# A linear-attention layer with an MLP on one core: batches 2 and 3 turn their first 384 tokens through memory, and their attention stands earlier in the order

## The chip, the cores and the metric

The kernel runs on one core of a Trainium2 chip. Time is device time in microseconds (us) of one execution. The core has TensorE (PE in the profile; its weight loads are PEld), VectorE (DVE), ScalarE (ACT), GpSimd (POOL), and SyncE (SP), whose only work here is to issue transfers.

## The reference, cut to what matters

```python
# r, k, v: (4, 8, 768, 48) f32; w, u: (8, 48)
for t in range(S):                                   # a state D x D for each batch and head
    cur = einsum('bhd,bhe->bhde', u[None] * kt, vt)
    y[:, :, t] = einsum('bhd,bhde->bhe', rt, state + cur)
    state = w[None, :, :, None] * state + einsum('bhd,bhe->bhde', kt, vt)
x = y.transpose(0, 2, 1, 3).reshape(4, 768, 384)
h = x.transpose(0, 2, 1) @ U @ V                     # U (768, 32), V (32, 768)
u = x + h.transpose(0, 2, 1)
out = u + maximum(u @ w_ch1, 0) @ w_ch2              # 384 -> 1536 -> 384
```

## The kernel before, in words

Each batch of 768 tokens is worked in six chunks of 128 tokens for the attention, and in two halves (t = 0 and 1) of 384 tokens for the MLP. The attention of batch b+1 runs between the matmuls of batch b's MLP, so that TensorE has work all the time.

**The order.** Every operation is given a key (a time in us, `at(t, f)`), and `Plan.schedule` (L152) walks through a modelled execution: on each engine it takes, among the operations whose inputs and buffers are ready by its own estimates, the one with the smallest key. The result is a fixed order for each engine, SyncE's queue among them; on the chip each engine works its list in that order and waits wherever an input is not there yet. `begin[b]` (L1456) is the key at which batch b's MLP begins, 49 x 1.85 apart. The MLP of a batch is 48 units of nine 384-wide matmuls, 1.85 apart in key (`mlp_units`, L1335): `m_1(f)` makes 128 of the 1536 hidden rows from u (L1257), ScalarE and VectorE split the result into a high and a low part (hh, hl), and `m_2(f)` (L1277) multiplies them with the second weights. For batches 1 to 3 the half t = 0 is done first (24 units), then t = 1.

**Attention.** `attention(b, t0, per, lead, step)` (L1473) gives chunk c the key t0 + per * c. For batches 2 and 3, t0 is begin[b-1] + 8 and per is 11, so that it ends at begin[b-1] + 74. Loads are keyed behind them: `a_load` (rows of r, k, v into tiles ldr, ldk, ldv, vsw) at the chunk's key less per and 16, `a_load_blocks` (r and k of three chunks as 32 x 32 blocks into tile bl, in runs of 128 bytes, 32 transfers) at the first chunk's key less per and 18. VectorE turns the blocks (L773), and scales them (L775, either VectorE or GpSimd). The chunk itself is `a_chunk` (L1050): products on TensorE whose first instruction is at L854; its two sums on VectorE make tile x, in token order.

**From attention to MLP.** `c_g(b)` (L1144) sums U against all six tiles x into Gs (32 rows, kept in three parts for accuracy), over TensorE, ScalarE and VectorE. What the MLP needs is u = x + h transposed, as a high part uTh and a low part uTl. There are two ways:

- *inside* (t = 0 of every batch, and t = 1 of batch 0): `c_x` (L1182) turns the three tiles x on TensorE against the identity into three PSUM banks (tiles pu, bank_sc, bank_tr), nine 128 x 128 transposes; `c_xu` (L1196) adds h to each bank by one matmul of Gs and V and splits the bank into uTh and uTl. Tile x stays without h, so that `m_2` of f = 0 adds h to the output by three more matmuls (*gates*, L1293).
- *through memory* (t = 1 of batches 1 to 3): `c_u` (L1168) makes h of one tile by one matmul and VectorE adds it to x; `c_store` (L1227) writes the tile to memory (tile ud) in runs of 128 bytes, so that 32 x 32 blocks stand turned; `c_blocks` (L1234) loads 128 rows of the turned array (tile ub); `c_turn` (L1240) turns the inside of the blocks on VectorE (tile ut) and splits into uTh and uTl. Both transfers are issued by SyncE.

The keys of both stand at the end of `rwkv_moe` (L1500 to L1532).

Of the kernel before, what the change touches and what calls it, by code (L numbers as in the profile page):

```python
# [47 lines left out]
class Plan:  # L48
# [33 lines left out]
    def op(self, eng, ns, fn, w=(), r=(), alt=(), lock=False, dma=0.0, rows=0, late=0.0, tiled=False, dk=0.0):  # L82


        if self.direct:
            fn()
            return None
        o = Op()
        o.n = len(self.ops)
        o.key = (self.key + dk, o.n)  # L90
        o.ways = [(eng, ns, fn, lock)] + list(alt)
        o.dma, o.rows, o.late, o.tiled = dma, rows, late, tiled
        o.deps, o.behind, o.allocs, o.bufs = set(), set(), [], []
        for acc, write in [(a, False) for a in r] + [(a, True) for a in w]:
            b, sub = acc if isinstance(acc, tuple) else (acc, None)
            if not b.uses and b.tag:
                o.allocs.append(b)
                ring = self.rings.setdefault(b.tag, {"order": [], "next": 0, "free": [(-99.0, "")] * b.bufs, "last": None})
                ring["order"].append(b)
            elif b.tag and b.uses[0][0] is not o:  # L100
                o.behind.add(b.uses[0][0])
            for p, s, pw in b.uses:
                if (write or pw) and (s is None or sub is None or s == sub) and p is not o:
                    o.deps.add(p)
            b.uses.append((o, sub, write))
            if b not in o.bufs:
                o.bufs.append(b)
                b.left += 1
        self.ops.append(o)
        return o  # L110
# [191 lines left out]
def rwkv_moe(ctx: ExitStack, tc: tile.TileContext, r, k, v, w, u, U, V, w1, w2, out):  # L302
    nc = tc.nc
    B, H, S, D = r.shape
    C = 128
    NCH = S // C
# [8 lines left out]
    NCT = DM // 128  # L315
# [3 lines left out]
    TPB = TB // 128  # L319
# [29 lines left out]
    def bank(tag, name):  # L349
        made = Buf(ps, [128, 512], F32, tag, {"mm": 2, "acc": 3}.get(tag, 1), name)  # L350
        if tag in ("tr", "sc"):
            if tag not in lasting:
                lasting[tag] = ps.tile([128, 512], F32, name=f"bank_{tag}", tag=tag, bufs=1)
            made.got = lasting[tag]
        return made
# [7 lines left out]
    def whole(*args, **kw):  # L363

        opened.clear()
        return nc.tensor.matmul(*args, **kw)  # L366

    def pe(ns, fn, w_, r_, tiled=False, dk=0.0):
        return op("PE", ns, fn, w_, r_, tiled=tiled, dk=dk)
# [16 lines left out]
    def dma(fn, w_, r_, rows, run, eng="SP", ns=470, dk=0.0, late=0.0, either=False):  # L386

        q = nc.scalar if eng == "ACT" else nc.sync
        return op(eng, ns, lambda: fn(q), w_, r_, dma=rows * max(1.05, run / 320),
                  rows=rows, late=late, dk=dk, alt=[("ACT", ns, lambda: fn(nc.scalar), False)] if either else ())  # L390
# [266 lines left out]
    xs = {}  # L657
# [510 lines left out]
    def c_u(b, i):  # L1168
        n = b * NCH + i

        pt = bank(("tr", "sc", "av")[i % 3], f"ph_{n}") if b < B else bank("mm", f"ph_{n}")
        pe(174, lambda: whole(pt.t[:, :DM], lhsT=V3.t[:, i * 128:(i + 1) * 128], rhs=Gs[b].t, start=True, stop=True),
           [pt], [V3, Gs[b]])
        on_dve(384, lambda e: e.tensor_tensor(xs[n].t, pt.t[:, :DM], xs[n].t, ALU.add), [xs[n]], [pt])
# [2 lines left out]

    def inside(b, t):

        return b < B and (t == 0 or b == 0)  # L1180

    def c_x(b, t, i):  # L1182

        if i == 0:
            upt[b, t] = [bank("acc" if (b, t) == (0, 0) else ("sc", "av", "tr")[ct], f"pu{b}_{t}_{ct}") for ct in range(NCT)]
        x = xs[b * NCH + t * TPB + i]
        for ct in range(NCT):
            pe(115, lambda ct=ct: whole(upt[b, t][ct].t[:, i * 128:(i + 1) * 128], lhsT=x.t[:, ct * 128:(ct + 1) * 128],
                                        rhs=ident_, start=(i == 0), stop=False, is_transpose=True, skip_group_check=True),
               [upt[b, t][ct]], [x])  # L1190
# [5 lines left out]
    def c_xu(b, t):  # L1196
        u_bufs(b, t)
        uh, ul = uT[b, t]
        for ct in range(NCT):
            pt = upt[b, t][ct]  # L1200
            pe(200, lambda ct=ct, pt=pt: whole(pt.t[:, :TB], lhsT=Gs[b].t[:, ct * 128:(ct + 1) * 128],
                                               rhs=V3.t[:, t * TB:(t + 1) * TB],
                                               start=False, stop=True, skip_group_check=True), [pt], [Gs[b], V3])
            on_act(384, lambda ct=ct, pt=pt: nc.scalar.copy(uh.t[:, ct, :], pt.t[:, :TB]), [(uh, ct)], [pt])
            on_dve(384, lambda e, ct=ct, pt=pt: e.tensor_tensor(ul.t[:, ct, :], pt.t[:, :TB], f32(uh.t[:, ct, :]),  # L1205
                                                                ALU.subtract), [(ul, ct)], [pt, (uh, ct)])
# [17 lines left out]
    ud_pool = ctx.enter_context(tc.tile_pool(name="ud", bufs=1, space=bass.MemoryType.DRAM))  # L1224
    ud = [Buf(ud_pool, [NCH, DM // 32, 32, 128], F32, None, 1, f"ud{b}") for b in range(B)]

    def c_store(b, i):  # L1227
        dma(lambda q: q.dma_start(ud[b].t[i].rearrange("k t (m c) -> (t m) k c", c=32),
                                  xs[b * NCH + i].t.rearrange("p (k c) -> p k c", c=32)), [(ud[b], i)], [xs[b * NCH + i]],
            1536, 128, ns=470)  # L1230

    ublk = {}

    def c_blocks(b, t, ct):  # L1234

        bt = ublk[b, t, ct] = wbuf([128, TPB, 128], F32, "xh", NXS, f"ub_{b}_{t}_{ct}")
        dma(lambda q: q.dma_start(bt.t, ud[b].t[t * TPB:(t + 1) * TPB, 4 * ct:4 * ct + 4].rearrange("j k t e -> (k t) j e")),
            [bt], [(ud[b], i) for i in range(t * TPB, (t + 1) * TPB)], 384, 512, late=1000)

    def c_turn(b, t, ct):  # L1240
        if ct == 0:
            u_bufs(b, t)
        uh, ul = uT[b, t]
        bt = ublk.pop((b, t, ct))
        ut = wbuf([128, TB], F32, "xl", NXS, f"ut_{b}_{t}_{ct}")
        on_dve(680, lambda e: e.transpose(ut.t.rearrange("p (j t m) -> p j m t", t=32, m=4),
                                          bt.t.rearrange("p j (m c) -> p j m c", c=32)), [ut], [bt])
        on_act(384, lambda: nc.scalar.copy(uh.t[:, ct, :], ut.t), [(uh, ct)], [ut])  # L1248
        on_either(384, lambda e: e.tensor_tensor(ul.t[:, ct, :], ut.t, f32(uh.t[:, ct, :]), ALU.subtract), [(ul, ct)],  # L1249
                  [ut, (uh, ct)])  # L1250
# [178 lines left out]
    def at(t, f):  # L1429
        steps.append((t, len(steps), f))  # L1430
# [25 lines left out]
    begin = [T0 + 49 * PER * b for b in range(B)]  # L1456
# [40 lines left out]
    end = attention(0, FRONT, EACH, 2.0, 0)  # L1497
    for i in range(3):
        at(end + 0.1 + 0.1 * i, lambda i=i: c_x(0, 0, i))
    for b in range(B):  # L1500
        n0 = b * NCH
        last = b + 1 == B
        t = begin[b]
        if b:
            t0, per = ((begin[b - 1] + 34, 8.0), (begin[b - 1] + 8, 11.0))[b > 1]
            for c in range(NCH):
                at(t0 + per * c - per - 16, lambda n=n0 + c: a_load(n))
            for c in range(0, NCH, 3):
                if turned(n0 + c):
                    continue  # L1510
                for i in (1, 3, 0, 2):
                    at(t0 + per * c - per - 18 + 0.1 * i, lambda n=n0 + c, i=i: (a_load_blocks(n, i, 0), a_load_blocks(n, i, 1)))
            end = attention(b, t0, per, 5.0, 0)
        at(end, lambda b=b: c_g(b))
        if b == 0:
            at(end + 0.9, lambda: again.append(pe(220, refill, [wk2], [xs[NCH - 1], V3])))
            at(end + 1, lambda: c_xu(0, 0))
            at(end + 1.5, lambda: again.append(pe(0, lambda: None, [wk2], [(uT[0, 0][1], NCT - 1)])))
            for i in range(TPB):
                at(t + 2 + 0.1 * i, lambda i=i: c_x(0, 1, i))  # L1520
            at(t + 3, lambda: c_xu(0, 1))
        else:
            for i in range(3):
                at(end + 0.1 + 0.1 * i, lambda b=b, i=i: c_x(b, 0, i))
            at(end + 1, lambda b=b: c_xu(b, 0))
            for i in (3, 4, 5):
                at(end + 2 + 0.3 * (i % 3), lambda b=b, i=i: (c_u(b, i), c_store(b, i)))
        for ct in range(NCT if b else 0):
            at(t + 2 + ct, lambda b=b, ct=ct: c_blocks(b, 1, ct))
            at(t + 16 + ct, lambda b=b, ct=ct: c_turn(b, 1, ct))  # L1530
        for j, f in enumerate(mlp_units(b)):
            at(t + PER * j, f)  # L1532
# [42 lines left out]
```

## Time and profile before

| | us |
|---|---|
| median of 3 runs | 411.86 (411.31 to 412.3) |
| the profiled execution | 412.28 |
| its span, first to last instruction | 410.5 |
| TensorE busy | 399.1 (97%) |
| VectorE busy | 266.2 (65%) |
| ScalarE busy | 130.9 (32%) |
| GpSimd busy | 87.6 (21%) |

The granted clock of TensorE is 0.996 of full speed on average. SyncE's queue moved 40.92 MB in 174606 packets, which took 49.5% of the time of the 16 DMA engines. In a row of the timeline the first number is the start from the span's begin, the second the length, then engine, line, operation, output<-inputs, partitions x elements and how many; a bracket names idle time before it and what ended it. L366 is the helper that issues every full-size matmul, so that there one goes by tiles: p is the MLP's bank, p<-uTh,w1s is m_1, p<-w2s,hh is m_2, p<-Gs,V a gate. L366 with bank_sc, ph or bank_tr<-Gs,V is c_u, with <-V,Gs c_xu, with <-ident,x c_x; L1136 is the sum of c_g.

### The profile page before, as it was taken

What the parts mean: (1) busy time and instruction counts of PE and PEld (TensorE: products, weight loads), DVE (VectorE), ACT (ScalarE), POOL (GpSimd) and SP (SyncE); (2) the same over time, 40 slices, a digit from 0 to 9 for tenths busy, and PEclk for the clock granted to TensorE, in tenths of its full rate; (3) what the DMA queues carried; (4) which work ended last, traced back from release to release, by engine and by line L of the source; (5) the groups of instructions that cost most, each with busy time, mean ns of one, the idle gap of its engine ahead of it and who ended that gap; (6) DMA issues with size and microseconds to landing.
All of it is one profiled execution on the core that took longest, in us unless ns stands there. A gap on an engine that the chain in (4) does not pass through costs nothing.

```text
span 410.5 us, 11500 instructions
## 1 busy us (share of the span) xinstructions
PE 399.1 (97%) x4801; PEld 383.1 (93%) x4801; DVE 266.2 (65%) x572; ACT 130.9 (32%) x349; POOL 87.6 (21%) x132
## 2 busy tenths in 40 slices
PE   6999899999999999999999999999999999999993
PEld 5898899999999899999999999999999999999993
DVE  5999999799998858876692478766422461131212
ACT  2688769474342312112012232011112221111110
POOL 4871521347425013321010012221000000000000
PEclk9999999999999999999999999999999999999998
DMA  8989796894459795945795854310100520001001
GB/s 166 187 243 222 117 280 135 202 271 86 73 84 185 120 196 88 169 80 96 139 157 87 123 133 74 69 31 16 47 2 2 90 85 0 2 0 61 0 1 62
DMA packets 178216, 42.89 MB, mean 104 GB/s; under 512 B 165229, under 2 KB 176622, under 8 KB 178158
## 3 DMA queue, kind: packets, MB, share of 16 engines
q1 hardware_dynamic: 174606, 40.92, 49.5%
q10 hardware_dynamic: 3552, 1.18, 1.1%
q8 instruction: 39, 0.64, 0.6%
q14 instruction: 19, 0.16, 0.2%
HBM read 35.59 MB, written 6.49 MB: 103 GB/s over the span
## 4 chain that ended last, share of the span: by engine, by line
PE 91%; DVE 5%; ACT 1%; issue 1%; POOL 0%; DVEq 0%; POOLq 0%
PE p L366 74%; PE pav L869 3%; PE pav L875 2%; PE pav L1022 1%; PE bank_tr L972 1%; PE bank_tr L829 1%; PE pav L1028 1%; PE bank_sc L829 1%; PE bank_tr L843 1%; PE bank_tr L1136 1%; PE pav L854 1%; PE bank_sc L843 1%; PE psu L994 1%; PE bank_tr L786 1%; DVE pw L485 1%
## 5 line engine op out<-in xcount | busy, mean ns | idle before, releaser
L366 PE MATMUL p<-uTh,w1s 128*128 128x384 f32 x576 | 148.9, 339 | 0.0
L366 PE MATMUL p<-w2s,hh 128*128 128x384 f32 x576 | 118.5, 336 | 0.0
L1272 ACT ACTIVATE hh<-p 128x384 fp32r<-128x384 f32 x96 | 47.2, 492 | 216.3 <-PE p L366 211.5
L1273 DVE SCALAR_TENSOR_TENSOR hl<-p,hh 128x384 fp32r<-128x384 f32 x96 | 53.1, 553 | 91.8 <-ACT hh L1272 91.3
L366 PEld LDWEIGHTS p<-uTh,w1s 128*128 128x128 f32 x576 | 102.7, 188 | 0.9
L366 PEld LDWEIGHTS p<-w2s,hh 128*128 128x128 f32 x576 | 101.0, 188 | 0.4
L366 PE MATMUL p<-uTl,w1s 128*128 128x384 f32 x288 | 96.6, 335 | 0.8 <-DVE uTl L1205 0.8
L366 PE MATMUL p<-w2s,hl 128*128 128x384 f32 x288 | 66.9, 334 | 0.0
L366 PEld LDWEIGHTS p<-uTl,w1s 128*128 128x128 f32 x288 | 54.0, 188 | 1.1 <-DVE uTl L1205 1.1
L366 PEld LDWEIGHTS p<-w2s,hl 128*128 128x128 f32 x288 | 51.5, 188 | 0.0
L738 POOL MEMSET ks<- 128x128 f32 x24 | 4.8, 204 | 104.5 <-PE bank_tr L843 102.2
L869 PE MATMUL pav<-ldv,am 64*64 64x48 f32 x288 | 20.8, 220 | 0.0
L875 PE MATMUL pav<-S,rT 48*64 48x48 f32 x528 | 20.1, 218 | 0.0
L869 PE MATMUL pav<-vsw,am 64*64 64x48 f32 x288 | 19.4, 220 | 0.0
L869 PEld LDWEIGHTS pav<-ldv,am 64*64 64x64 f32 x288 | 18.0, 134 | 1.0 <-issue 0.8
L1108 DVE TENSOR_TENSOR S<-bank_tr,SW 112x192 f32<-112x192 f32 x15 | 5.3, 355 | 20.7 <-PE bank_tr L843 20.7
L1313 DVE TENSOR_TENSOR x<-p,x 128x384 f32<-128x384 f32 x30 | 14.9, 547 | 5.7 <-PE p L366 5.4
L869 PEld LDWEIGHTS pav<-vsw,am 64*64 64x64 f32 x288 | 17.5, 134 | 1.0 <-issue 1.0
L875 PEld LDWEIGHTS pav<-S,rT 48*64 48x64 f32 x528 | 18.0, 135 | 0.0
L584 DVE SCALAR_TENSOR_TENSOR raw_w<-raw_w 128x384 int32<-128x384 int32 x24 | 15.4, 656 | 0.1
L748 POOL TENSOR_TENSOR dv<-ldr,ldk 128x384 f32<-128x384 f32 x12 | 12.8, 1063 | 11.7 <-DMA bl<-in_r_dram 6.6
L1249 POOL TENSOR_TENSOR uTl<-ut,uTh 128x384 fp32r<-128x384 f32 x3 | 3.0, 1015 | 54.0 <-ACT uTh L1248 54.0
(192 smaller groups left out, 593.5 us busy)
## 6 DMA issues: line engine op xcount, KB each, us to landing
raw_w<-in_moe_w_ch_dram SPq DMA_DIRECT2D x24, 384.0 KB, 5.0
out_dram<-x SPq DMA_DIRECT2D x21, 192.0 KB, 1.9
ldr<-in_r_dram SPq DMA_DIRECT2D x20, 192.0 KB, 3.4
ldk<-in_k_dram SPq DMA_DIRECT2D x20, 192.0 KB, 3.9
ldv<-in_v_dram SPq DMA_DIRECT2D x20, 192.0 KB, 4.2
bl<-in_r_dram SPq DMA_DIRECT2D x79, 48.0 KB, 2.9
bl<-in_k_dram SPq DMA_DIRECT2D x79, 48.0 KB, 2.4
vsw<-in_v_dram SPq DMA_DIRECT2D x36, 48.0 KB, 3.1
```

The lines of the kernel that those rows point to most:

```text
L366: return nc.tensor.matmul(*args, **kw)
L584: nc.vector.scalar_tensor_tensor(word(0), word(1), 3, word(0), ALU.logical_shift_left, ALU.bitwise_or)
L738: op("POOL", 250, lambda: nc.gpsimd.memset(ks.t[:, :, D:], 0.0), [(ks, "pad")], [])
L748: on_either(384, lambda e, a_=a_, b_=b_: e.tensor_mul(dv.t, a_()[:, :, :D], b_()[:, :, :D]), w_, r_, only="POOL" if front(n) else None)
L829: return [lambda q=q, i=i: nc.tensor.matmul(pt.t[(i ^ j) * C2:(i ^ j) * C2 + C2, q * C2:(q + 1) * C2], lhsT=kT.t[rows, q, i * C2:(i + 1) * ...
L843: return nc.tensor.matmul(pt.t[j * HP:j * HP + D, SU + q * D:SU + (q + 1) * D], lhsT=ks.t[half, 2 * q + j, :D], rhs=vt()[half, 2 * q + j, ...
L869: return nc.tensor.matmul(to(q, j, i), lhsT=am[j].t[half, q, :], rhs=vsw[n].t[half, q, :] if j else vt()[half, 2 * q, :], start=((i == 1 i ...
L875: return nc.tensor.matmul(to(q, row, i), lhsT=rT.t[rows, q, i * C2:(i + 1) * C2], rhs=St[n, i].t[rows, q, :], start=False, stop=((alone or ...
L1108: on_dve(192, lambda e, new=new, ptv=ptv, dec=decayed[n, j]: e.tensor_tensor(new.t, ptv(), dec.t, ALU.add), [new], [pt, decayed[n, j]])
L1272: on_act(384, lambda: nc.scalar.activation(hh.t, pt.t[:, :TB], AF.Relu), [hh], [pt])
L1273: on_dve(384, lambda e: e.scalar_tensor_tensor(hl.t, pt.t[:, :TB], 0.0, f32(hh.t), ALU.max, ALU.subtract), [hl], [pt, hh])
L1313: on_dve(384, lambda e, x=x, pt=pt: e.tensor_tensor(x.t, pt.t[:, :DM], x.t, ALU.add), [x], [pt])
```

## The change

Batches 2 and 3 have no half *inside* any more: their first 384 tokens go through memory too, by c_u, c_store, c_blocks and c_turn with keys right behind c_g. Their attention gets t0 = begin[b-1] + 5 and per = 10, and so ends at begin[b-1] + 65. The second half's c_u and c_store come at end + 8 instead of end + 2, and the stores of its tiles 4 and 5 are each issued as two transfers of 64 partitions. Batches 0 and 1 keep their ways and keys.

```diff
     def inside(b, t):
-        return b < B and (t == 0 or b == 0)
+        return b < 2 and t <= 1 - b
...
-    def c_store(b, i):
-        dma(lambda q: q.dma_start(ud[b].t[i].rearrange("k t (m c) -> (t m) k c", c=32),
-                                  xs[b * NCH + i].t.rearrange("p (k c) -> p k c", c=32)), [(ud[b], i)], [xs[b * NCH + i]],
-            1536, 128, ns=470)
+    def c_store(b, i, parts=1):
+        m = 128 // parts
+        for j in range(parts):
+            dma(lambda q, j=j: q.dma_start(ud[b].t[i].rearrange("k t (m c) -> (t m) k c", c=32)[j * m:(j + 1) * m],
+                                           xs[b * NCH + i].t.rearrange("p (k c) -> p k c", c=32)[j * m:(j + 1) * m]),
+                [(ud[b], (i, j))], [xs[b * NCH + i]], 12 * m, 128, ns=470)
...
-            [bt], [(ud[b], i) for i in range(t * TPB, (t + 1) * TPB)], 384, 512, late=1000)
+            [bt], [(ud[b], (i, j)) for i in range(t * TPB, (t + 1) * TPB) for j in range(2)], 384, 512, late=1000)
...
-            t0, per = ((begin[b - 1] + 34, 8.0), (begin[b - 1] + 8, 11.0))[b > 1]
+            t0, per = ((begin[b - 1] + 34, 8.0), (begin[b - 1] + 5, 10.0))[b > 1]
...
-            for i in range(3):
-                at(end + 0.1 + 0.1 * i, lambda b=b, i=i: c_x(b, 0, i))
-            at(end + 1, lambda b=b: c_xu(b, 0))
+            if inside(b, 0):
+                for i in range(3):
+                    at(end + 0.1 + 0.1 * i, lambda b=b, i=i: c_x(b, 0, i))
+                at(end + 1, lambda b=b: c_xu(b, 0))
+            else:
+                for i in range(TPB):
+                    at(end + 0.2 + 0.1 * i, lambda b=b, i=i: (c_u(b, i), c_store(b, i)))
+                for ct in range(NCT):
+                    at(end + 1 + 0.1 * ct, lambda b=b, ct=ct: c_blocks(b, 0, ct))
+                    at(end + 5 + ct, lambda b=b, ct=ct: c_turn(b, 0, ct))
             for i in (3, 4, 5):
-                at(end + 2 + 0.3 * (i % 3), lambda b=b, i=i: (c_u(b, i), c_store(b, i)))
+                at(end + (8 if b > 1 else 2) + 0.3 * (i % 3), lambda b=b, i=i: (c_u(b, i), c_store(b, i, parts=2 if b > 1 and i > 3 else 1)))
```

## The prediction

> **What bounds the kernel now.** I read the page first (engines, then the chain that ended last), then busy time by stretch, then TensorE's own order in the timeline around the passage from one batch to the next, and last SyncE's queue there.
>
> ```profile
> span 410.5 us, 11500 instructions
> PE 399.1 (97%) x4801; PEld 383.1 (93%) x4801; DVE 266.2 (65%) x572; ACT 130.9 (32%) x349; POOL 87.6 (21%) x132
> PE 91%; DVE 5%; ACT 1%; issue 1%; POOL 0%; DVEq 0%; POOLq 0%
> ```
>
> The first two lines say that TensorE (PE) is never short of work, the third that the chain of work that ended last runs over PE for 91% of the span. By stretch (length, then busy time and instructions of PE, its weight loads, VectorE (DVE), ScalarE and GpSimd, the granted clock, DMA share, GB/s):
>
> ```profile
> 72.00:135.00 63.00, 63.00 (x1044) 59.25 (x1046) 56.88 (x122) 28.93 (x83) 30.31 (x34) 1.00 0.71 151
> 146.00:212.00 66.00, 66.00 (x1052) 63.92 (x1051) 50.87 (x113) 10.69 (x24) 12.97 (x21) 1.00 0.73 130
> 221.00:229.00 8.00, 7.85 (x89) 7.06 (x88) 4.31 (x10) 3.12 (x8) 0.00 (x0) 1.00 0.39 56
> 239.00:305.00 66.00, 66.00 (x1052) 64.08 (x1052) 42.57 (x96) 12.62 (x32) 9.61 (x16) 1.00 0.25 52
> ```
>
> While a batch's attention runs between the MLP of the batch before (146 to 212 for batch 2, 239 to 305 for batch 3) PE has no gap, and its clock is granted in full (1.00). So in these stages time is the sum of PE's instructions: one removed is time won, unless something makes PE wait. From 72 to 135 DVE is busy 56.88 of 63 us and PE still has no gap: a DVE at 90% does not hold PE up here.
>
> **What goes from PE.** PE's order at the passage from batch 1 to batch 2, the matmuls on tile p between, and the time at which Gs is complete:
>
> ```profile
> 221.20 1.20 PE L1136 MATMUL bank_tr<-x,Uf 128*32 128x96 f32 x48
> ...
> 224.30 0.34 PE L366 MATMUL p<-uTl,w1s 128*128 128x384 f32 x1
> 224.78 0.41 PE L366 MATMUL bank_sc<-V,Gs 96*128 96x384 f32 x1 [0.15 <-DVE Gs L1164]
> ...
> 226.62 0.34 PE L366 MATMUL bank_sc<-Gs,V 96*128 96x384 f32 x1
> ...
> 235.83 0.51 PE L366 MATMUL p<-uTh,w1s 128*128 128x384 f32 x2
> 236.18 0.33 PE L366 MATMUL p<-uTl,w1s 128*128 128x384 f32 x1
> 236.35 0.51 PE L366 MATMUL p<-uTh,w1s 128*128 128x384 f32 x2
> ...
> 240.03 0.79 PE L366 MATMUL p<-Gs,V 96*128 96x384 f32 x3
> ```
> ```profile
> 222.30:235.80 13.50, 11.90 (x63) 11.05 (x64) 1.78 (x4) 1.51 (x3) 1.00 0.72 108
> 315.10:328.60 13.50, 11.87 (x63) 11.02 (x64) 1.75 (x4) 1.51 (x3) 1.00 0.41 74
> ```
> ```profile
> 224.09 0.56 DVE Gs L1164
> ```
>
> A 384-wide matmul advances PE by 0.52 / 3 = 0.1735 us (235.83 to 236.35 for three). At 235.83 batch 2's MLP begins, two m_1 ahead of its gates. Between c_g's sums and that point lie 13.50 us with 63 matmuls of the MLP of batch 1, or 10.93 us. The other 2.57 us are the nine transposes (c_x), the three matmuls of c_xu, three of c_u, and a wait: 224.30 + 0.17 = 224.47, but the first c_xu starts at 224.78, because Gs is done only at 224.65. Batch 3 has the same 13.50 and 63, so the same 2.57.
>
> Removed in each of batches 2 and 3: 2.57 less the three c_u that stay (0.52) = 2.05 us, and the three gate matmuls of the first tile (the row at 240.03), 0.52. Added: three c_u for tokens 0 to 383, 0.52. The gates and the new c_u cancel. The wait of 0.31 I let stand: a c_u now comes first behind Gs as c_xu did before, so it can wait as long. That leaves 2.05 - 0.31 = 1.74 us per batch, **3.5 us in all**; if the wait went too, 4.1.
>
> **What goes to DVE, ScalarE and the queue, and how far ahead it has to be.** The new operations exist already for the second 384 tokens, so their prices are rows:
>
> ```profile
> L1246 DVE STREAM_TRANSPOSE ut<-ub 128x384 f32<-128x384 f32 x9 | 7.4, 858 | 0.0
> L1248 ACT CAST uTh<-ut 128x384 fp32r<-128x384 f32 x9 | 4.5, 509 | 5.8 <-DVE ut L1246 5.8
> L1249 DVE TENSOR_TENSOR uTl<-ut,uTh 128x384 fp32r<-128x384 f32 x6 | 3.2, 553 | 0.6 <-ACT uTh L1248 0.6
> L1174 DVE TENSOR_TENSOR x<-bank_tr,x 128x384 f32<-128x384 f32 x3 | 1.6, 545 | 0.0
> ```
> ```profile
> out_dram<-x SPq DMA_DIRECT2D x21, 192.0 KB, 1.9
> ud<-x SPq DMA_DIRECT2D x9, 192.0 KB, 3.5
> ub<-ud SPq DMA_DIRECT2D x9, 192.0 KB, 3.0
> ```
> ```profile
> 220.50 5.15 SPq L728 DMA_DIRECT2D bl<-in_r_dram  x8
> 228.65 2.01 SPq L1228 DMA_DIRECT2D ud<-x  x3
> ...
> 233.59 0.37 SPq L1237 DMA_DIRECT2D ub<-ud  x1
> 236.26 2.37 SPq L1318 DMA_DIRECT2D out_dram<-x  x3
> 238.68 1.04 SPq L1237 DMA_DIRECT2D ub<-ud  x2
> ```
>
> DVE gets three adds and three block transposes per batch, 3 x 0.545 + 3 x 0.858 = 4.2 us; ScalarE's three casts and the three subtractions only change their source. With the attention packed closer, the 50.87 us of DVE work of the stretch 146 to 212 fall into some 8 us less, 50.87 / 58 = 88%: under the 90% that cost nothing above. I cost it at nothing; the cover is that DVE's result hl is needed only after six matmuls of its unit.
>
> The wait that is added: the first m_1 of the MLP of batches 2 and 3 now needs data that went to memory and back, and behind that m_1 everything on PE queues, for no other batch has MLP work then. The trip, from c_g's start: Gs after 224.65 - 221.20 = 3.45; first c_u to first store 228.65 - 226.62 = 2.03, with 0.1 for the start 5.6; store issue to first block load 233.59 - 228.65 = 4.94; the third load issued 1.0 later, landing 3.0; then transpose, cast and subtraction 0.86 + 0.51 + 0.55 = 1.9, and 0.5 for one DVE operation ahead. Sum 17.0 us.
>
> What it has: today c_g starts 235.83 - 221.20 = 14.6 us ahead, with 63 / 9 = 7 units of the MLP behind it; that would not do. The new keys end the attention at begin + 5 + 60 = 65 instead of 74; at 1.85 per unit c_g comes after unit 35, and 12 units stand behind it: 108 matmuls, 18.7 us, plus c_g 1.1 and six c_u 1.0, together **20.9 us**. Margin 3.9 us; nothing is late by these rows. The other end: if the first store stands behind one group of eight block loads (5.15 us, the row at 220.50), the trip takes 22.2 us and lacks 1.3. I take 17.0, because the first half's transfers have the smaller keys and the order puts them first as soon as x is ready.
>
> The same key changes pull the chunks of attention up by 3 us (first) to 8 us (last) and their loads by 2 to 7 us. On SyncE's in-order queue (SP) the first half's three stores and three loads pass ahead of loads of the next batch's blocks (as in the row at 220.50); a store waiting there for DVE's add holds those loads back, for at most the 2 us above, and they are wanted a chunk later. The second half's stores, 6 us later in the order and with two more issues, feed an MLP half that begins 24 units, 37 us, after the first: nothing.
>
> The trip's price has one page against it. The Trainium skill (DMA: Bandwidth & Descriptors, section Rules for kernel authors) says to transpose by the hardware DMA transpose and not by a plain DMA with a rearranged access pattern, and gives a "19× difference". Its estimate: 19 x 1.9 = 36 us for a store, 29 us of stall in each batch, some 466 us in all. The rows do not bear it out: the same 192 KB land in 3.5 us in 128-byte runs and in 1.9 us as output rows, 1.8 times, because DVE does the inner 32 x 32 turn. I take the 3.5.
>
> **Rivals.**
>
> *A. Small stalls (17%).* The order is fixed beforehand from estimated times; pulled up, a chunk may be issued before its inputs are there.
>
> ```profile
> 175.91 0.20 PE pav L854
> ...
> 199.02 0.20 PE pav L854
> ```
> ```profile
> 171.82 1.32 POOL L739 TENSOR_TENSOR ks<-ldk,tab 128x384 f32<-128x384 f32 x1 [2.11 <-DMA ldk<-in_k_dram]
> 184.02 0.67 DVE L775 TENSOR_TENSOR rT<-rT,tabT 112x512 f32<-112x512 f32 x1
> ```
>
> The row at 171.82 shows a load that landed 2.1 us later than its place in the order expected; today it ends at 173.14, in front of the chunk of 175.91. Batch 2's third chunk moves up by 5 us, to 171, and a landing so late could then stop PE: 408.4 + 2.1 = 410.5 us. Against it: the last chunk's operands (184.02) are ready 14 us before the chunk of 199.02 reads them, and a chunk that the order itself sees as late is merely put behind more MLP.
>
> *B. The transposes were only filler (5%).* If PE had to wait for Gs anyway, they cost nothing and only c_xu is won: 2 x 0.52 = 1.0 us, 410.8. Against it: MLP matmuls stand between them (224.30), and 12 more units will be there.
>
> *C. The trip is not covered: slower (10%).* If batch 2's attention cannot move up because its loads hold it (DMA is 0.73 busy from 146 to 212), c_g stays 7 units ahead instead of 12. The trip then lacks 5 x 9 x 0.1735 - 3.9 = 3.9 us at the first m_1: 408.4 + 3.9 = 412.3; with batch 3 the same, 416.2. It decides against the change once the trips together overrun by more than 3.5 us. The queue can do this too: the three loads today were issued over 239.72 - 233.59 = 6.1 us instead of 1.4, because an output store that waited for DVE stood between; that delay at the first half is 4.7 us, more than the margin. Against it: the first half's loads have lower keys than any output store near them, and batch 3 has DMA at 0.25. By the page above it would be C at its worst, which I give less than 1%.
>
> **How the numbers follow.** The profiled execution took 412.28 us, 0.42 above the median of three, 411.86 (411.31 to 412.3). Its span of 410.5 would become 407.0; taken from the median, 411.86 - 3.5 = **408.4 us**, chance 66%, own range 407.2 (with the wait gone 407.8, less the 0.55 by which the lowest run lies under the median) to 409.3 (0.44 by which the highest run lies over it, and half a microsecond of waits). About 0.2% (0.8 us) is what a measurement of this kernel can tell. A and B reach up to 410.8, which I take as the upper end; 407.2 to 410.8 leaves out C and a few per cent. Faster by more: the forecast, nearly all of A, half of B, 0.83. Same: 0.07 (the other half of B, A doubled, a small C). Slower: 0.10.
>
> **What would show it.** In the profile of the changed kernel: nine transposes on pu, bank_sc and bank_tr and the gates gone from batches 2 and 3, three c_u more each; c_g at some 213 and 305; 108 matmuls of p between it and the next batch's first m_1; 19 stores (four tiles in two parts) and 15 loads on ud; no idle time of PE on uTh or uTl at MLP begin. The forecast is wrong if PE's idle time beyond 45 us grows by more than 1 us, or if the first m_1 waits for ub or ut (C), or a chunk for ks, kT or rT (A).

## The result, and the profile after

| | before | after |
|---|---|---|
| median | 411.68 us of 4 runs (411.31 to 412.3) | 407.8 us of 4 runs (407.48 to 408.39) |
| the profiled execution | 412.28 us | 408.04 us |

The ratio is 0.9906, with a 95% interval of 0.9888 to 0.9924: 3.9 us won, where 3.5 had been predicted (408.4 us, range 407.2 to 410.8).

From the page of the kernel after: span, busy time of the engines, and the chain that ended last.

```profile
span 406.2 us, 11508 instructions
PE 395.9 (97%) x4777; PEld 380.4 (94%) x4777; DVE 270.4 (67%) x577; ACT 134.3 (33%) x361; POOL 93.2 (23%) x137
PE 93%; DVE 4%; issue 1%; ACT 1%; POOL 0%; DVEq 0%; POOLq 0%
```

TensorE is still the bound. It has 24 instructions and 3.2 us of work less (4801 to 4777, 399.1 to 395.9); VectorE has 4.2 us more (266.2 to 270.4), and the chain shows none of it. The waits of TensorE in the kernel after of 0.6 us and more (engine, tile and line, the releaser; us in total, times, longest):

```profile
PE wake L366 <- POOL ident masks.py:199: 1.8, 1, 1.8
PE ptk L786 <- DVE ks L739: 1.1, 1, 1.1
PE p L366 <- DVE uTl L1205: 0.8, 1, 0.8
PE pt_tabf L470 <- DVE back L489: 0.6, 1, 0.6
```

These are waits of the kernel's begin and of batch 0 (L1205 is the split of the *inside* way), and the kernel before has the same ones to within 0.1 us. The list has two more of 0.4 us each, both before 82 us. None is on uTh or uTl of lines 1250 and 1251, the operands that now come through memory. The passage from batch 1 to batch 2 in TensorE's timeline after:

```profile
213.42 1.20 PE L1136 MATMUL bank_tr<-x,Uf 128*32 128x96 f32 x48
...
216.56 0.34 PE L366 MATMUL p<-uTl,w1s 128*128 128x384 f32 x1
217.00 0.41 PE L366 MATMUL bank_tr<-Gs,V 96*128 96x384 f32 x1
...
234.29 0.68 PE L366 MATMUL p<-w2s,hl 128*128 128x384 f32 x3
234.81 0.51 PE L366 MATMUL p<-uTh,w1s 128*128 128x384 f32 x2
...
236.20 0.34 PE L366 MATMUL p<-uTl,w1s 128*128 128x384 f32 x1
```

No transpose and no c_xu stands there any more. c_g starts at 213.42 (213 was predicted), the first m_1 of batch 2 at 234.81, straight behind the last m_2 of batch 1 (234.29 + 0.52 = 234.81). The sum Gs still ends a short gap: 216.56 + 0.17 = 216.73, and the first c_u starts at 217.00.

Against the kernel before: the first m_1 of batch 1 stands at 142.99 before and 143.01 after, that of batch 2 at 235.83 and 234.81, that of batch 3 at 328.66 and 326.07, and the last matmul starts here:

```profile
403.89 0.34 PE L366 MATMUL p<-w2s,hl 128*128 128x384 f32 x1
```
```profile
400.78 0.34 PE L366 MATMUL p<-w2s,hl 128*128 128x384 f32 x1
```

(The first row is of before, the second of after.) Up to batch 2's MLP 1.04 us are won, up to batch 3's 1.57 more, and behind it 0.52, the three gates of batch 3: together 3.1 us. The spans differ by 4.3. The other 1.2 us lie behind the last matmul, 410.5 - 403.9 = 6.6 us before and 406.2 - 400.8 = 5.4 after, where the last output is added and stored, which the change does not touch. That stretch scatters between executions: over the twelve kernels of this document it takes 5.3 to 6.6 us, and 6.5 in one that differs from the changed kernel only in the key of its second half's stores. So the traces show 3.1 us of the change; the 3.9 of the medians have an interval of 3.1 to 4.6 us (the ratios 0.9924 and 0.9888).

The trip through memory in the kernel after, first SyncE's queue (start, time over which so many transfers were issued), then VectorE:

```profile
218.04 2.18 SPq L1230 DMA_DIRECT2D ud<-x  x3
...
222.76 1.54 SPq L1230 DMA_DIRECT2D ud<-x  x2
224.48 1.58 SPq L1239 DMA_DIRECT2D ub<-ud  x3
```
```profile
229.29 0.56 DVE L1275 SCALAR_TENSOR_TENSOR hl<-p,hh 128x384 fp32r<-128x384 f32 x1 [2.56 <-ACT hh L1274]
229.77 1.55 DVE L1248 STREAM_TRANSPOSE ut<-ub 128x384 f32<-128x384 f32 x2
231.19 0.56 DVE L1251 TENSOR_TENSOR uTl<-ut,uTh 128x384 fp32r<-128x384 f32 x1
231.67 0.87 DVE L1248 STREAM_TRANSPOSE ut<-ub 128x384 f32<-128x384 f32 x1
...
233.12 0.56 DVE L1251 TENSOR_TENSOR uTl<-ut,uTh 128x384 fp32r<-128x384 f32 x1
```

The last uTl is done at 233.12 + 0.56 = 233.68, so the trip takes 233.68 - 213.42 = 20.3 us, where 17.0 had been predicted. It has 234.81 - 213.42 = 21.4 us (predicted 20.9). By the prediction's count, from the last uTl to the first m_1, the margin is 1.1 us and not 3.9. In batch 3 the trip is 20.3 us and the margin 1.1 too. This count is stricter than the order needs: the first m_1 is nine matmuls, three for each block, and only the ninth, the row at 236.20, reads the last uTl, 2.5 us after it is done. So the time came out as forecast, on a thinner cover than the forecast had counted on. That is what most of the experiments are about.

### The profile page after: what moved, and what is told of

The parts are those of the page before. It is cut to its first block, busy times and chain, and to the rows that moved or that the text cites. A ratio compares the mean times of both kernels' runs of the same rounds, so it can differ in the third digit from the quotient of the medians.

```text
span 406.2 us, 11508 instructions
## 1 busy us (share of the span) xinstructions
PE 395.9 (97%) x4777; PEld 380.4 (94%) x4777; DVE 270.4 (67%) x577; ACT 134.3 (33%) x361; POOL 93.2 (23%) x137
## 4 chain that ended last, share of the span: by engine, by line
PE 93%; DVE 4%; issue 1%; ACT 1%; POOL 0%; DVEq 0%; POOLq 0%
PE p L366 76%; PE pav L869 3%; PE pav L875 2%; PE pav L1022 1%; PE bank_tr L972 1%; PE bank_tr L829 1%; PE pav L1028 1%; PE bank_sc L829 1%; PE bank_tr L843 1%; PE bank_tr L1136 1%; PE pav L854 1%; PE bank_sc L843 1%; PE psu L994 1%; PE bank_tr L786 1%; PE wake L366 1%
## 5 line engine op out<-in xcount | busy, mean ns | idle before, releaser
L1251 POOL TENSOR_TENSOR uTl<-ut,uTh 128x384 fp32r<-128x384 f32 x7 | 7.1, 1017 | 75.6 <-ACT uTh L1250 75.6
L869 PE MATMUL pav<-vsw,am 64*64 64x48 f32 x288 | 19.5, 220 | 0.0
L1315 DVE TENSOR_TENSOR x<-p,x 128x384 f32<-128x384 f32 x30 | 14.9, 546 | 4.3 <-PE p L366 4.0
L748 POOL TENSOR_TENSOR dv<-dv,ub 128x384 f32<-128x384 f32 x10 | 12.3, 1236 | 16.8 <-DVE dv L748 15.6
L759 ACT ACTIVATE dv<-ldv,dg 128x48 f32<-128x48 f32 x56 | 13.4, 321 | 4.9 <-DVE dg L755 4.9
```

Of the source, the lines that this page charges most:

```text
L748: on_either(384, lambda e, a_=a_, b_=b_: e.tensor_mul(dv.t, a_()[:, :, :D], b_()[:, :, :D]), w_, r_, only="POOL" if front(n) else None)
L759: nc.scalar.activation(dv.t[:, h], vt()[:, h], AF.Copy, scale=dg.t[:, h:h + 1])
L869: return nc.tensor.matmul(to(q, j, i), lhsT=am[j].t[half, q, :], rhs=vsw[n].t[half, q, :] if j else vt()[half, 2 * q, :], start=((i == 1 i ...
L1315: on_dve(384, lambda e, x=x, pt=pt: e.tensor_tensor(x.t, pt.t[:, :DM], x.t, ALU.add), [x], [pt])
```

## The experiments

Theory T: TensorE's order is the bound, the change is worth the instructions that it takes from that order, and the nearer place of the attention does nothing but cover the trip. The rivals are those of the prediction (B: the transposes were only filler; C: the trip is not covered), and one more, D: the new place itself wins the time, whatever way the tokens take. The first four kernels ran on one chip (before 411.95 us, median of 23 runs), the next four on another (411.62, of 21), the last two on a third (411.19, of 11). Ratios are to the kernel before on the same chip.

### The old place, with the way through memory

```diff
-            t0, per = ((begin[b - 1] + 34, 8.0), (begin[b - 1] + 5, 10.0))[b > 1]
+            t0, per = ((begin[b - 1] + 34, 8.0), (begin[b - 1] + 8, 11.0))[b > 1]
```

> The changed kernel with the attention of batches 2 and 3 where it was (begin + 8, 11 apart). Theory 'price and cover' (the gain is TensorE's removed matmuls, the new place of the attention is only the cover of the trip through memory, which took 20.3 us from the start of c_g to the last uTl in the changed kernel): c_g comes 7 units ahead of the MLP, which is 1.1 + 10.9 + three or six c_u (0.5 or 1.0) + 0.3 = 12.8 to 13.3 us; the first m_1 waits for 7.0 to 7.5 us in each batch, 4 at least if the trip shrinks to the 17.0 of the prediction; time 415 to 423 us, slower than the kernel before (411.7). Rival 'the order finds its own way' (the schedule puts the transfers ahead of everything and the trip is hidden anyway): 407.8.

Measured: 418.52 us (417.7 to 419.75), ratio 1.0147 (1.0097 to 1.0198): slower than the kernel before by 6 us and than the changed one by 10.7. The wait of TensorE that heads its list, the rows at the first m_1 of batch 2, and four stretches of 3.41 us around the two waits (the columns are those of the prediction's table by stretch):

```profile
PE p L366 <- ACT uTh L1250: 5.6, 2, 3.1
```
```profile
240.65 0.62 PE L366 MATMUL p<-uTh,w1s 128*128 128x384 f32 x2 [3.06 <-ACT uTh L1250]
241.74 0.64 PE L366 MATMUL p<-uTl,w1s 128*128 128x384 f32 x1 [0.47 <-POOL uTl L1251]
...
243.14 0.84 PE L366 MATMUL p<-uTh,w1s 128*128 128x384 f32 x2
...
244.10 0.84 PE L366 MATMUL p<-uTh,w1s 128*128 128x384 f32 x2
```
```profile
238.40:241.82 3.42, 0.70 (x3) 0.38 (x3) 3.42 (x9) 1.37 (x3) 1.54 (x2) 1.00 0.72 204
241.82:245.23 3.41, 3.41 (x11) 3.41 (x12) 2.17 (x5) 1.57 (x6) 0.00 (x0) 0.50 0.83 199
333.97:337.39 3.42, 1.39 (x6) 1.09 (x7) 3.35 (x6) 1.06 (x3) 0.68 (x1) 1.00 1.11 278
337.39:340.80 3.41, 3.41 (x12) 3.35 (x12) 1.96 (x4) 1.46 (x3) 0.35 (x1) 0.50 0.62 180
```

This is the prediction's C, at the place that it named: the first m_1 of each MLP waits for the data that came through memory. The waits are less than half of the 7.0 to 7.5 us expected. The first m_1 can start as soon as the high part of the first block is there, 240.60 - 222.69 = 17.9 us after c_g's start and 16.4 in batch 3, and need not wait for the last uTl, which is done 19.9 and 18.9 us after it.

An exposed wait also costs more than its length. The waits on uTh sum to 5.6 us, and behind each the granted clock is 0.50 for 3.41 us: three matmuls advance TensorE by 244.10 - 243.14 = 0.96 us instead of 0.52, so that 1.7 us more are lost in each batch, 3.4 us in all. With the 0.47 us on uTl these are 9.5 of the 10.7 us; the rest was not traced to a cause. That the time still lies in the expected 415 to 423 us is luck: the waits had been counted too long (4 us at least in each batch), and the slow clock not at all. The Trainium skill (TensorE: Matmul & The Clock Gate, section Part 1: The HAM clock gate) says that the clock goes to half after an idle window of some 3.4 us and comes back after as long a busy one, the windows running free. The trace agrees on the half clock and on the 3.41 us, and the two falls lie 337.39 - 241.82 = 95.57 us apart, 28 times 3.413. But the window before a fall was not idle: TensorE was busy for 0.70 us of it in batch 2 and for 1.39 us in batch 3.

### The new place alone

```diff
     def inside(b, t):
-        return b < 2 and t <= 1 - b
+        return b < B and (t == 0 or b == 0)
...
-                at(end + (8 if b > 1 else 2) + 0.3 * (i % 3), lambda b=b, i=i: (c_u(b, i), c_store(b, i, parts=2 if b > 1 and i > 3 else 1)))
+                at(end + 2 + 0.3 * (i % 3), lambda b=b, i=i: (c_u(b, i), c_store(b, i, parts=1)))
```

> The kernel before with only the new place of the attention (begin + 5, 10 apart); the first halves of batches 2 and 3 are still turned on TensorE. 'Price and cover': the place costs and wins nothing, 411.7 within 0.5. Rival 'the place is part of the gain' (less crowding of VectorE and of the loads before the MLP): 409 to 410.5. A third way, the place costs small stalls that the shorter TensorE work paid for: 412.5 or more.

Measured: 411.39 us (410.66 to 413.53), ratio 0.9989 (0.9965 to 1.0013). In its trace the stretches from one batch's first m_1 to the next take 92.89 and 92.87 us, where the kernel before has 92.84 and 92.83. D falls: the place without the new way is worth nothing that can be told from zero. With the run before it, each half of the change alone is level or slower, and only both together win.

### A place in between

```diff
-(begin[b - 1] + 5, 10.0))[b > 1]
+(begin[b - 1] + 5, 10.5))[b > 1]
```

> The changed kernel with the chunks of batches 2 and 3 10.5 apart instead of 10, so that the attention ends 3 key-us, one or two units, nearer to the MLP. The cover shrinks from 21.4 us to 18.3 to 19.8. If the trip needs the 20.3 us that it took in the changed kernel: waits of 0.5 to 2.0 us in each batch at the first m_1, 408.8 to 411.8. If it needs only the 17.0 of the prediction and stretched because there was time: no wait, 407.8 within 0.5.

Measured: 408.93 us (407.55 to 414.1), ratio 0.9928 (0.9898 to 0.9958), not to be told from the changed kernel's 0.9906. The trace has no wait on uTh or uTl. The planner reacts: with attention ending 3 us later in its keys, c_g starts at 214.33 and 305.77, counted from batch 1's first m_1 only 1.6 and 1.7 us later than in the changed kernel. A key that asks for less cover does not get less in proportion. In batch 3 the cover is 325.26 - 305.77 = 19.5 us, and the last uTl is done at 326.26, a microsecond after the first m_1 has started; still nothing waits, because the matmul that reads it starts at 327.17. So the margin of 1.1 us is not the distance to a cliff.

### The second half's stores later

```diff
-                at(end + (8 if b > 1 else 2) + 0.3 * (i % 3), ...
+                at(end + (20 if b > 1 else 2) + 0.3 * (i % 3), ...
```

> The changed kernel with c_u and the stores of the second half at end + 20 instead of end + 8, behind the first half's block loads. My reading of the longer trip is that the second half's stores stood between the first half's stores and loads on SyncE's queue and shared the DMA engines: then store issue to first block load falls from 6.4 and 7.1 us to about 4.9, the trip from 20.3 to about 17 us, the time stays at 407.8 within 0.5 because the trip is covered either way. Rival: the second half has nothing to do with it (the transfers of 128-byte runs and the loads of the next batch's blocks make it): the trip stays at 20 us, at least in batch 2.

Measured: 408.1 us (407.21 to 409.65), ratio 0.9897 (0.9858 to 0.9936): no difference, as both sides had it. What was to be decided stands in the trace. In the changed kernel the second half's two stores (the row at 222.76 above) go ahead of the first half's block loads, and the way from first store to first load is 224.48 - 218.04 = 6.4 us, 7.1 in batch 3. Here:

```profile
218.66 2.06 SPq L1230 DMA_DIRECT2D ud<-x  x3
...
223.94 1.47 SPq L1239 DMA_DIRECT2D ub<-ud  x3
```
```profile
229.39 0.56 DVE L1275 SCALAR_TENSOR_TENSOR hl<-p,hh 128x384 fp32r<-128x384 f32 x1 [2.56 <-ACT hh L1274]
229.86 1.55 DVE L1248 STREAM_TRANSPOSE ut<-ub 128x384 f32<-128x384 f32 x2
```

From store to load it is now 5.3 us (5.0 in batch 3), as expected. But the transposes start at 229.86 as they did at 229.77: the time won in the queue is lost again on VectorE, and the trip takes 20.4 and 20.0 us. My reading that the second half's stores lengthen the trip is right for the queue and wrong for the trip. VectorE works its list in order, the transposes stand behind a split hl, and that split waits 2.56 us for ScalarE and TensorE.

### The old place, with the second half's stores later

```diff
-(begin[b - 1] + 5, 10.0))[b > 1]
+(begin[b - 1] + 8, 11.0))[b > 1]
...
-                at(end + (8 if b > 1 else 2) + 0.3 * (i % 3), ...
+                at(end + (18 if b > 1 else 2) + 0.3 * (i % 3), ...
```

> E1 (attention of batches 2 and 3 where it was, so that the trip through memory is exposed) with c_u and stores of the second half at end + 18 instead of end + 8. In E1 the trip took 18.8 us in batch 3 and 19.8 in batch 2 with TensorE waiting for it, and two or more stores of the second half stood between the first half's stores and loads. 'The second half's stores lengthen the trip by their 1.5 to 2.5 us': the trip falls to 17 to 17.5 us, the time by 3 to 5 us to 414 to 415.5. 'They only fill time in which the loads wait anyway': the trip stays at 19 to 20 and the time at 418.5.

Measured: 420.12 us (418.97 to 420.43), ratio 1.019 (1.0164 to 1.0215): not the 414 to 415.5 of the first reading, and by the intervals not to be told from the 1.0147 of the old place (1.0097 to 1.0198). From store to load it fell to 5.1 and 5.3 us, and the trip did not shorten: 20.3 and 19.8 us, where the old place had 19.9 and 18.9. VectorE in batch 3 of this kernel, around the transposes:

```profile
333.83 0.55 DVE L1174 TENSOR_TENSOR x<-bank_tr,x 128x384 f32<-128x384 f32 x1
...
334.76 0.54 DVE L1174 TENSOR_TENSOR x<-ph,x 128x384 f32<-128x384 f32 x1
335.23 1.53 DVE L1248 STREAM_TRANSPOSE ut<-ub 128x384 f32<-128x384 f32 x2
```

The second half's three adds, moved back, now stand right in front of the first half's transposes and hold them back by 335.23 - 333.83 = 1.4 us. What is put off on one engine's list lands in front of something else there.

### The transposes put back as dead work

The changed kernel, with the nine transposes of c_x issued in batches 2 and 3 and their result unused; nothing else is changed.

```diff
             else:
+                for i in range(3):
+                    at(end + 0.1 + 0.1 * i, lambda b=b, i=i: c_x(b, 0, i))
                 for i in range(TPB):
```

> The changed kernel with the nine transposes of the first half put back in batches 2 and 3 as dead work: c_x turns the three tiles into the banks as before and nothing reads them. It prices the transposes alone. 'Price': 2.05 - 0.31 - 3 x 0.1735 = 1.22 us per batch, 2.4 in all, 410.2 us. Rival B of the prediction, 'they were only filler in front of Gs': no change, 407.8.

Measured: 410.3 us (409.26 to 415.42), ratio 0.9957 (0.9937 to 0.9977): against the changed kernel's 0.9906 that is 2.1 us more, and the two intervals do not touch. In the trace each stretch from one first m_1 to the next is 1.0 us longer than in the changed kernel (92.81 us for 91.80, 92.31 for 91.26), where 1.22 had been expected. Rival B, by which they fill time that TensorE would wait anyway, said 407.8 and falls: TensorE's time here is the sum of what it is given. The transposes cost some two of the four microseconds that the change won.

### Batch 3 alone

```diff
     def inside(b, t):
-        return b < 2 and t <= 1 - b
+        return b < 2 and t <= 1 - b or b == 2 and t == 0
```

Batch 2's attention and the second half of its tokens go back to their old keys with it.

> Only batch 3 goes through memory and has the new place; batch 2 is as in the kernel before. 'Price': half of the gain, 1.6 to 2.0 us under the kernel before, about 409.9. Rival: the gain sits in one batch, 407.8 or 411.7.

Measured: 410.02 us (409.49 to 412.36), ratio 0.9956 (0.9927 to 0.9985). From batch 2's first m_1 to the last matmul its trace is 1.6 us shorter than the kernel before, 166.5 us for 168.1. One batch brings about half of the two batches' gain.

### Batch 1 too

```diff
     def inside(b, t):
-        return b < 2 and t <= 1 - b
+        return b < 1
...
-            t0, per = ((begin[b - 1] + 34, 8.0), (begin[b - 1] + 5, 10.0))[b > 1]
+            t0, per = ((begin[b - 1] + 24, 7.0), (begin[b - 1] + 5, 10.0))[b > 1]
```

The second half of batch 1's tokens gets the later key of batches 2 and 3 with it.

> The changed kernel with batch 1's first half through memory as well, its attention at begin[0] + 24, 7 apart (before 34 and 8). 'Price and cover': one more batch at 1.6 to 2.0 us, 406.0, if its attention can be packed so close. Against it: in the stretch 88 to 120 of the changed kernel VectorE is busy 15.46 and 15.89 of 16 us, and batch 1's attention and the conversion of the weights share it; then TensorE waits for VectorE and the time is 408 to 414.

Measured: 416.89 us (416.38 to 423.44), ratio 1.0117 (1.0087 to 1.0147), slower than either case expected. c_g of batch 1, the first m_1 behind it, and VectorE's time (fourth column) in batch 1's attention; the last fence is the same stretch of the changed kernel:

```profile
135.98 1.20 PE L1136 MATMUL bank_tr<-x,Uf 128*32 128x96 f32 x48
...
151.14 1.01 PE L366 MATMUL p<-uTh,w1s 128*128 128x384 f32 x2 [5.55 <-ACT uTh L1250]
```
```profile
88.00:104.00 16.00, 16.00 (x264) 15.09 (x263) 15.73 (x35) 9.44 (x23) 5.78 (x7) 1.00 0.98 241
104.00:120.00 16.00, 16.00 (x250) 15.00 (x248) 15.87 (x34) 9.28 (x25) 10.32 (x9) 1.00 0.75 132
```
```profile
88.00:104.00 16.00, 16.00 (x278) 14.84 (x280) 15.46 (x35) 7.43 (x21) 10.27 (x10) 1.00 0.60 128
104.00:120.00 16.00, 16.00 (x320) 15.03 (x312) 15.89 (x35) 7.84 (x25) 7.87 (x12) 1.00 0.53 83
```

Asked to end some 16 us earlier, batch 1's attention ends no earlier at all: c_g stands at 135.98, and at 134.89 in the changed kernel. VectorE was full there already (15.46 and 15.89 of 16 us). So the trip has too little cover, 151.14 - 135.98 = 15.2 us with the wait itself, and C comes with one wait of 5.55 us. VectorE's time is the likely limit for batch 1. It is not shown to be the only one: the DMA share of the first stretch rose from 0.60 to 0.98 with the change, and the two were not separated. One place for batch 1 was tried; others are open.

### The transposes earlier in VectorE's list, at the old place and at the new

The planner adds 1 us of its own to the landing of a block (`late`). In both kernels this is taken away for the first half of batches 2 and 3, in the first at the old place of the attention, in the second in the changed kernel:

```diff
-            [bt], [...], 384, 512, late=1000)
+            [bt], [...], 384, 512, late=0 if b > 1 and t == 0 else 1000)
```

> The changed kernel with the attention of batches 2 and 3 at its old place, as in the run with the old place (418.52 us, waits of 5.6 us on the high part of the turned tokens), and one number of the written order changed: the order's own estimate of when a block of the first 384 tokens lands is 1 us earlier, so that VectorE's list takes the three transposes of these blocks sooner. If it is the place in VectorE's list that ends the trip (my theory: in batch 2 of the run with the old place the first transpose ran at 239.22, the three block loads were issued from 233.44 to 235.05, and no block load took more than 3.5 us to land), the trip falls from 19.9 and 18.9 us by 0.5 to 1 us in both batches and the time to 416.5 to 418. If the landing of the loads or the queue ends it, the transposes wait for the load at their new place, nothing comes earlier, and the time stays 418.5 (417.7 to 419.8) or is a little longer.

Measured: 417.52 us (416.43 to 418.22), ratio 1.0153 (1.0131 to 1.0175). The ratio says no more than the 1.0147 of the old place; the trace decides, and it decides by halves. In batch 2 the trip fell from 19.9 to 19.0 us and the wait on uTh from 3.06 to 2.21; in batch 3 it stayed at 18.9, because there the transposes stand behind three adds of L1315 that wait for TensorE. The waits sum to 4.7 us instead of 5.6. Behind the two of them the clock does not do the same. Four stretches of 3.41 us, the first two around the wait in batch 2, the others over that in batch 3:

```profile
236.83:240.25 3.42, 1.25 (x6) 0.93 (x7) 3.42 (x8) 1.92 (x6) 1.84 (x2) 1.00 0.68 198
240.25:243.66 3.41, 3.41 (x12) 3.41 (x12) 2.58 (x7) 1.02 (x4) 0.00 (x0) 0.50 0.79 179
328.99:332.41 3.42, 2.35 (x14) 2.03 (x12) 1.73 (x4) 0.00 (x0) 0.00 (x0) 1.00 0.91 213
332.41:335.82 3.41, 1.95 (x9) 1.46 (x10) 2.83 (x6) 1.54 (x3) 1.02 (x1) 1.00 0.97 248
```

After 2.21 us of waiting it fell to 0.50, after 2.53 us in batch 3 it stayed at 1.00, from 335.82 on too. The stretches are cut where the clock changed, and on in steps of the same length. The shorter wait lies in one of them and leaves TensorE 1.25 us busy; the longer is split between two and leaves 2.35 and 1.95. The traced execution is also the fastest of the five (416.43 us at a mean clock of 0.995; the others 417.33 to 418.22 us at 0.987 to 0.988).

> The same number changed in the changed kernel itself, with its attention at the new place. There the trip (20.3 us) lies under other work (21.4 us), so by either theory the time stays where it is: 407.8 us, ratio to the kernel before 0.988 to 0.993. If the place in VectorE's list ends the trip, the transposes come 0.5 to 2 us earlier than 229.77 and 321.1 us, and the margin ahead of the MLP grows from 1.1 us by as much; if the landing does, they stay within 0.3 us of these times.

Measured: 408.0 us (407.33 to 408.7), ratio 0.9918 (0.9897 to 0.9939), level with the changed kernel. VectorE in batches 2 and 3:

```profile
227.00 2.25 DVE L1248 STREAM_TRANSPOSE ut<-ub 128x384 f32<-128x384 f32 x3 [0.89 <-DMA ub<-ud]
229.09 0.55 DVE L1275 SCALAR_TENSOR_TENSOR hl<-p,hh 128x384 fp32r<-128x384 f32 x1
229.55 1.47 DVE L1251 TENSOR_TENSOR uTl<-ut,uTh 128x384 fp32r<-128x384 f32 x2
...
319.25 2.27 DVE L1248 STREAM_TRANSPOSE ut<-ub 128x384 f32<-128x384 f32 x3 [1.88 <-DMA ub<-ud]
321.36 0.55 DVE L1275 SCALAR_TENSOR_TENSOR hl<-p,hh 128x384 fp32r<-128x384 f32 x1
321.82 1.00 DVE L1251 TENSOR_TENSOR uTl<-ut,uTh 128x384 fp32r<-128x384 f32 x2
```

The transposes now stand ahead of the split hl, 2.8 and 1.8 us earlier (0.6 us of it because this execution reached c_g that much sooner), and here VectorE does wait for the block loads (the brackets). The trip falls from 20.3 us to 231.02 - 212.80 = 18.2 and to 322.82 - 304.07 = 18.8, and the margins ahead of the MLPs (234.19 and 325.45) grow from 1.1 to 3.2 and 2.6 us. So the place in VectorE's list was worth 1.5 to 2.1 us of the trip, and the time did not move: cover beyond what is needed is worth nothing.

## Why the prediction was right, point by point

- **TensorE is the bound, and an instruction that goes is time won: shown.** The dead transposes cost their time again (2.1 us), one batch brings half of the gain, and the place alone brings nothing.
- **The removed work.** Up to the last matmul 3.1 us were won, against a term of 3.5. By batch: 1.04 (predicted 1.74 less the 0.52 of the gates, that is 1.22), then 1.57 (1.74), then the 0.52 of the last gates. Each batch gave 0.2 us less than counted. The dead transposes show where: nine of them cost 1.0 us a batch, and the prediction's remainder, 2.57 us less the wait and six matmuls, had left 1.22 for them. The medians differ by 3.9; what goes beyond 3.1 is no more than the scatter of the executions, so that 3.9 lies so near 3.5 is in part luck.
- **Gates and new c_u cancel; the wait for Gs stays.** The gap in front of the first c_u is 0.27 us in batch 2 and 0.26 in batch 3, against 0.31 before. Choosing to let it stand was right: with 4.1 instead of 3.5 the forecast would have been further from the trace.
- **The cover.** 20.9 us predicted, 21.4 measured: 108 matmuls, six c_u, c_g and the gap.
- **The trip is the term that was mis-sized,** 17.0 us predicted and 20.3 measured. c_g to first store took 218.04 - 213.42 = 4.6 (predicted 5.6). First store to first load took 6.4 (4.9), because two of the second half's stores slipped in between; the prediction had put these "6 us later in the order ... nothing", and only their own MLP half, not the first half's loads behind them, had been looked at. First load to the last uTl took 233.68 - 224.48 = 9.2 (1.0 + 3.0 + 1.9 + 0.5 = 6.4), because VectorE's list held the transposes behind a split; "0.5 for one DVE operation ahead" counted the operation's length and not its wait of 2.56 us. The margin of 3.9 shrank to 1.1, and the forecast held because it was still above zero. That an error of 3.3 us stayed inside 3.9 was luck, for nothing in the prediction bounded it. One choice worked the other way: the trip was counted to the last uTl, but held against the start of the first m_1, which reads the last uTl only with its ninth matmul.
- **The transfers' price.** A store of 192 KB landed in 3.3 us (median) where 3.5 was taken, a block load in 3.1 (3.0). Output stores of the same 192 KB took 2.0 us, so the stores in 128-byte runs cost 1.7 times as much, and the prediction's estimate of 36 us is refuted. The page's 19 is stated against the hardware DMA transpose, which no run here has, so that factor itself was not measured.

```profile
out_dram<-x SPq DMA_DIRECT2D x21, 192.0 KB, 2.0
ub<-ud SPq DMA_DIRECT2D x15, 192.0 KB, 3.1
ud<-x SPq DMA_DIRECT2D x11, 192.0 KB, 3.3
ud<-x SPq DMA_DIRECT2D x8, 96.0 KB, 3.3
```

- **VectorE and the stretch of the attention.** 45.21 of 59 us from 146 to 205, and TensorE without a gap (59.00). Costing the adds and the transposes at nothing was right for time.
- **A (small stalls):** no chunk of batches 2 and 3 waits in the trace after. **B (filler):** refuted by the dead transposes. **C (trip not covered):** a true mechanism whose condition did not arise here. At the old place it does, and its price was set too low: 416.2 us predicted for both batches, 418.52 measured. The waits on uTh came out shorter than counted (5.6 us, against 3.9 in each batch); the slow clock behind them, 3.4 us, had not been counted.

## What to carry to other kernels

When the bound engine has no gaps, count the instructions that leave its list; then look for the one new wait that could open a gap, and compare the length of that trip with the work behind which it runs. In the length of a trip, an operation in front on an in-order engine counts with its own wait, not only with its duration, and every transfer that shares the queue counts, also those meant for later. A margin needs to be positive and no more: making it larger moved nothing, and the engine that sets how far work can be pulled ahead (here, it seems, VectorE in batch 1) decides where the same change stops paying.

## What the hardware showed that was not expected

- Once it is full, TensorE's granted clock is either 1.00 or 0.50, and in each of the twelve traces it changes only on a grid of 3.41 us. In the kernel at the old place it falls at 9.71, 241.82 and 337.39 us, and these are 68 and 28 times 3.413 us apart. How long TensorE was busy in the step before decides. In all twelve traces every step with at most 1.66 us of work was followed by one at half speed, and no step with 1.8 us or more was. So it is not the length of a wait that counts but how it falls on the grid: 2.21 us in one step were enough, 2.53 us split between two were not. A wait of 3 us in dense work therefore costs from 3 to nearly 5 us.
- The same happens at a kernel's begin, by chance from one execution to the next. In three of the traces the step from some 6.5 to 10 us had 1.55 to 1.63 us of work, the next ran at half speed, and batch 0's MLP began at 45.0 to 45.1 us instead of 43.9 to 44.0.
- Half a tile, 96 KB from 64 partitions, lands no sooner than a whole one of 192 KB: 3.3 us both (medians of 8 and 11 stores).
